# Splitting the loop of expert units in two: w_in in eight units, w_out three tiles at a time, and ten w_out tiles converted in the first token pair

## The chip, the cores and the metric

One core of one Trainium2 chip runs the whole program in one launch. The metric is the device time of one execution in microseconds. Before the change, three runs took 1532.82, 1535.92 and 1537.63 us, median 1535.92 us. The execution that was profiled took 1532.53 us, of which 1530.8 us lie between the first and the last instruction of the program.

## The reference, cut to what matters

The program computes three layers in sequence on 4608 tokens of width 512:

```python
x = attention(q, k, v)                 # keys and values averaged over 8 positions first
e = argmax(x @ w_gate + bias[modality])            # one of 8 experts for each token
x = gate * (relu(x @ w1[e]) @ w2[e])               # w1: 512x1024, w2: 1024x512, float32
h = x @ w_in                                       # w_in: 512x2048
out = (h * clip(h + 3, 0, 6) / 6) @ w_out          # w_out: 2048x512
```

`w_in` and `w_out` are float64 in memory. The kernel multiplies numbers as the sum of a high and a low float32 part with three products (high*high, high*low, low*high). So each float64 weight has first to be turned, with integer and float operations on its two 32-bit words, into two such parts. This is the conversion that the change moves about.

## The kernel before, in words

The work runs in three stages one after the other: the attention, which also routes each token's row to a list of its expert in device memory; the expert units (function `moe1`); and the last layer (function `moe2`).

An expert unit is 400 rows of one expert. The inputs of this case make twelve units. The first (`unit(0, first=True)`) and the last (`unit(..., last=True)`) are written out, the ten between them are one hardware loop whose count is read from a register (`nc.values_load(g.nun, ...)`, L1040, `tc.For_i`, L1041). A unit has eight steps `f`. Step `f` issues the load of the weight tile `f+3` (`w_dma`, L880 and L882, two transfers of 256 KB into one of two buffers `ws`), splits tile `f+2` into high and low parts (`w_split`: a cast `wh` on ACT and a subtraction `wl` on DVE, twice), multiplies tile `f` with the unit's rows (`h_mm`, 12 matmuls into `ph`, then `hi` on ACT and `lo` on DVE), and then the second product of the tile before (`y_mm`, 12 matmuls into `y`; every third of them reads `lo`). Steps 1 to 4 load the next unit's rows, POOL scales them one step later (`gate_x`, L863). In step 7 and behind it four column blocks of these rows are transposed on PE into `pt` and split into `xhi` (ACT) and `xlo` (DVE); the first block's bank also holds the tokens' numbers, which ACT copies to `tkr` (L876). `pt` has two banks, so the third transpose waits for the readers of the first: `xhi`, `xlo` and `tkr`.

Beside this, each of the ten loop units converts weights for the last layer. `conv` turns one half of a column chunk of `w_in` (`cs`, two transfers of 256 KB) into the seven sums `wq` of a Strassen scheme, in 13 operations, 2 of them on ACT and 11 on DVE; `conv_out` turns one of the sixteen tiles of `w_out` (`ds`, 512 KB) into `wv`, in 9 operations, 2 on ACT and 7 on DVE. A unit does two `conv` and one `conv_out`, 35 operations, handed out in order, five behind each of the steps 1 to 7:

```python
for _ in range(5):
    if ops:
        ops.pop(0)()
```

The results go to device memory: `wq` by L931 behind steps 4 and 6, `wv` by L1029 behind step 7. Which chunk and which tile a unit takes stands in rows 3 and 4 of the table `g.tab`: `min(i, 7)` for the chunk of `w_in` (there are eight, `NQ = 8`), `min(i, 9)` for the tile of `w_out` (`KD = 10`). With ten loop units the chunk 7 is therefore converted three times. These numbers are read into SP's registers at the start of a unit (L973, L974).

The last layer takes the tokens in six pairs of blocks (`j`), each in eight quads (`q`, one for each chunk of `w_in`). A quad (`quad`) has seven products `mm` of six matmuls into one of two PSUM banks `hps`, and between them the output matmuls (`o_group`, 36 in all) of the quad before; `rest(i)` behind product `i` issues what `extra[i]` holds, the next load of `sq` (`s_load`, 256 KB, seven ahead) and one or two of those groups. DVE adds what the Strassen scheme asks for (`vv`, `ww`, `c`) and makes `gl`; a product that goes on in a bank, or takes it anew, waits until DVE has read it. In the first pair (`j == 0`) one of the six `w_out` tiles that the loop did not convert is converted in each of the quads 0 to 5 (nine operations over `extra[0]` to `extra[4]`), and the other ten are fetched from device memory (`wo_get`, 512 KB each).

The order on PE, ACT, DVE and SP is the order in which the program text issues the operations; each engine works its queue in order, and SP issues nearly all transfers. An operation that waits holds up what stands behind it on its engine. A loop has no barrier between its iterations, but when it ends all engines wait for each other and SP waits for the loop's transfers.

Of the kernel before, what the change touches and what calls it, by code (L numbers as in the profile page):

```python
# [8 lines left out]
F32 = mybir.dt.float32  # L9
# [10 lines left out]
P = 128  # L20
# [21 lines left out]
KD = 10  # L42
# [612 lines left out]
def unit_consts(tc, g, c1):  # L655
# [29 lines left out]
    cv = f("ucv", 40)  # L685
    nc.gpsimd.tensor_scalar(cv[0:1], cw[0:1], float(KD - 1), None, op0=ALU.min)
    nc.gpsimd.tensor_scalar(cw[0:1], cw[0:1], float(NQ - 1), None, op0=ALU.min)
    g.tab = g.cp.tile([1, 5, 40], I32, name="tab")
# [3 lines left out]
    nc.gpsimd.tensor_copy(g.tab[:, 4, 1:40], cv[0:1, 0:39])  # L692
# [61 lines left out]
def unit_table(tc, g, new):  # L754
# [9 lines left out]
    v.tensor_scalar(g.nun, u.m[0:1], -2.0, None, op0=ALU.add)  # L764
# [49 lines left out]
def moe1(tc, g, xr_d, tok_d, y_d, s_d, v_d, w1, w2, w_in):  # L814
# [83 lines left out]
    def store_y(col):  # L898
        return nc.sync.dma_start(y_d.rearrange("(d p) n -> p d n", p=P)[:, :, bass.ds(col, NW)], s.yo)
# [25 lines left out]
    def conv_out(t):  # L925
        a, m, ex = (s.cv.tile([P, 4, P], I32, name=n, tag=n).rearrange("p k f -> p (k f)") for n in ("a", "m", "ex"))
        o = s.cv.tile([P, 2, DM], F32R, name="wv", tag="wv")
        return o, f64_split(nc, g, t[:, :, 1], t[:, :, 0], a, m, ex, o[:, 0], o[:, 1])
# [4 lines left out]
    def unit(i, first=False, last=False, tail=None):  # L933
# [29 lines left out]
        for f in range(8):  # L963
# [6 lines left out]
            if f == 0 and not first:  # L970
                col = reg(2, i, NT)
                if not last:
                    cc = nc.values_load(g.tab[0:1, 3, bass.ds(i, 1)], engines=(ET.SP,), min_val=0, max_val=NQ - 1)  # L973
                    cd = nc.values_load(g.tab[0:1, 4, bass.ds(i, 1)], engines=(ET.SP,), min_val=0, max_val=KD - 1)  # L974
# [20 lines left out]
            if last:  # L995
                if f in (1, 2):
                    g.y_load(0, f - 1)
                if f == 3:
                    ops = g.y_ops(0)
                if f >= 3:  # L1000
                    g.s_load()
                    for _ in range(3):
                        if ops:
                            ops.pop(0)()
                if f >= 6:
                    g.wo_load(KD + f - 6)
            elif not first:
                if f == 0:
                    cs[0], cs[1] = conv_load(cc, 0), conv_load(cc, 1)
                if f == 1:  # L1010
                    co, ops = conv(cs.pop(0))
                if f == 2:
                    cs[2] = g.wo_load(cd)
                if f == 3:
                    c1_, o_ = conv(cs.pop(1))
                    ops += o_
                if f == 5:
                    c2_, o_ = conv_out(cs.pop(2))
                    ops += o_
                for _ in range(5):  # L1020
                    if ops:
                        ops.pop(0)()
                if f == 4:
                    conv_store(co, cc, 0)
                if f == 6:
                    conv_store(c1_, cc, 1)
                if f == 7:
                    assert not ops
                    nc.sync.dma_start(v_d[bass.ds(cd, 1)].rearrange("o p x -> p (o x)"), c2_.bitcast(F32).rearrange("p w f -> p (w f)"))  # L1029
# [7 lines left out]
    def run(tail):  # L1037
        open_ps()
        unit(0, first=True, tail=tail)
        n_l = nc.values_load(g.nun, min_val=10, max_val=18)  # L1040
        with tc.For_i(0, n_l, 1, iteration_sync="reg_based") as i:  # L1041
            unit(i + 1)
        unit(n_l + 1, last=True)
        store_y(reg(2, n_l + 2, NT))
        es_p.close()
        es_l.close()
        es_r.close()
# [6 lines left out]
def moe2(tc, g, tok_d, v_d, out):  # L1054
# [23 lines left out]
    def wo_get(f):  # L1078
        nc.sync.dma_start(wo[f].bitcast(F32).rearrange("p w f -> p (w f)"), v_d[f])  # L1079
# [57 lines left out]
    def quad(j, q, groups, extra):  # L1137
# [29 lines left out]
        x = bank()  # L1167
# [20 lines left out]
    wo_get(NQ)  # L1188
    groups = []
    yo = []  # L1190
    for j in range(NP):
        for q in range(NQ):
            extra = {i: [] for i in range(7)}
            if j == 0:
                if q < KF - KD:
                    for n, op_ in enumerate(conv(KD + q)):
                        extra[n // 2].append(op_)
                if q < KF - KD - 2:
                    extra[6].append(lambda q=q: g.wo_load(KD + q + 2))
                for f in (q + 1, NQ + q + 1):  # L1200
                    if q < NQ - 1 and f < KD:
                        extra[3 if f < NQ else 4].append(lambda f=f: wo_get(f))
                if q == 1:
                    extra[0].append(lambda: v.tensor_copy(tki, tkf))  # L1204
            if j + 1 < NP:
# [23 lines left out]
def chunk_kernel(ctx, tc, q, k, v, mid, w_gate, mbias, w1, w2, w_in, w_out, out):  # L1229
# [7 lines left out]
    v_d = dp.tile([KD, P, 2 * DM], F32, name="vd")  # L1237
    s_d = dp.tile([NQ, 7, 2, P, 2 * P], F32, name="sd")
    with tc.manual_schedule(engines={ET.PE, ET.Activation, ET.DVE, ET.SP}):
# [50 lines left out]
        def wo_load(f):  # L1290
            t = g.yp.tile([P, DM, 2], I32, name="ds", tag="ds", bufs=2)
            src = w_out.bitcast(I32).rearrange("(f p) x -> f p x", p=P)[bass.ds(f, 1)]
            nc.sync.dma_start(t.rearrange("p f w -> p (f w)"), src.rearrange("o p x -> p (o x)"))
            if isinstance(f, int):
                g.sts[f] = t
            return t
# [36 lines left out]
```

## Time and profile before

| | |
|---|---|
| runs | 1532.82, 1535.92, 1537.63 us |
| profiled execution | 1532.53 us, span 1530.8 us |
| PE busy | 1421.2 us (93%) |
| DVE busy | 978.9 us (64%) |
| ACT busy | 624.2 us (41%) |
| POOL busy | 206.9 us (14%) |
| first transpose of a unit's tokens, ten loop units apart | 248.3 and 699.1 us |
| last layer's first product | 747.6 us |

PE is busy for most of the span in every stage, so a stretch is read by what PE waits for in it and at which clock it ran. The granted clock is given as a share: 1.00 is 2.4 GHz, 0.5 is 1.2 GHz.

### The profile page before, as it was taken

The page shows a single profiled execution, that of the slowest core. Times are in us where ns is not written, and L with a number is a line of the kernel's source. Part 1 is how long each engine was busy: PE and PEld are TensorE (multiplying, and loading weights), DVE is VectorE, ACT ScalarE, POOL GpSimd, SP SyncE. Part 2 cuts the span into 40 slices and gives each one's busy share as a digit, 9 for nine tenths or more (in the row PEclk, how much of TensorE's full clock was granted, in tenths as well). Part 3 has the DMA queues.
Part 4 walks back from the last instruction along what each step waited for, and adds up shares of the span by engine and source line. Part 5 has one row for each costly group of instructions (what it writes and reads, how often), then busy time and mean ns, then how long its engine had stood idle before and what let it go on. Part 6 is the DMA issues. An engine that isn't in the chain of part 4 may idle for free.

```text
span 1530.8 us, 24942 instructions
## 1 busy us (share of the span) xinstructions
PE 1421.2 (93%) x7673; PEld 1289.5 (84%) x7673; DVE 978.9 (64%) x1964; ACT 624.2 (41%) x1263; POOL 206.9 (14%) x233
## 2 busy tenths in 40 slices
PE   7898988889888889888899999999999999999998
PEld 6787877888888888888888888888888888888886
DVE  7898773877777887776667644554564464455443
ACT  3665643444444444344433433333343243333322
POOL 5654242111100111110000010010010001001001
PEclk8999998999999999999999999999999999999999
DMA  9973254776766677765775454355445335445442
GB/s 297 287 230 127 97 165 128 221 236 220 233 196 210 204 233 229 237 211 183 236 257 162 127 176 142 113 152 159 117 138 173 116 118 172 138 117 152 118 116 69
DMA packets 243142, 268.29 MB, mean 175 GB/s; under 512 B 25762, under 2 KB 203426, under 8 KB 243058
## 3 DMA queue, kind: packets, MB, share of 16 engines
q1 hardware_dynamic: 235858, 247.04, 53.1%
q0 software_dynamic: 7200, 20.18, 3.6%
q8 instruction: 47, 0.77, 0.2%
q14 instruction: 37, 0.30, 0.1%
HBM read 213.55 MB, written 61.01 MB: 179 GB/s over the span
## 4 chain that ended last, share of the span: by engine, by line
issue 48%; PE 3%; POOL 2%; DMA 0%; SPq 0%; POOLq 0%; ACT 0%; DVE 0%
POOL out_dram L1092 2%; PE ph L945 1%; PE y L958 1%; DMA sq<-sd 0%; SPq L1283 0%; PE hps L1113 0%; POOLq L1328 0%; SPq L1079 0%; ACT dex L795 0%; POOLq L1092 0%; ACT s L1153 0%; SPq L1184 0%; DVE dm L796 0%; DVE tki L1204 0%
## 5 line engine op out<-in xcount | busy, mean ns | idle before, releaser
L1113 PE MATMUL hps<-yc,sq 128*128 128x384 f32 x2016 | 412.6, 339 | 11.7 <-DVE c L1134 6.6
L1113 PEld LDWEIGHTS hps<-yc,sq 128*128 128x128 f32 x2016 | 364.1, 188 | 47.3 <-DVE c L1134 13.7
L1103 PE MATMUL ops<-wo,gh 128*128 128x512 f32 x1152 | 361.5, 394 | 0.0
L1103 PEld LDWEIGHTS ops<-wo,gh 128*128 128x128 f32 x1152 | 212.4, 187 | 22.9
L1103 PE MATMUL ops<-wo,gl 128*128 128x512 f32 x576 | 227.9, 396 | 0.0
L787 DVE TENSOR_TENSOR wl<-ws,wh 128x512 fp32r<-128x512 f32 x192 | 139.3, 755 | 77.1 <-ACT wh L786 69.0
L1124 ACT ACTIVATE r<-c,three 128x384 f32<-128x384 f32 x144 | 88.8, 617 | 220.0 <-DVE c L1134 219.0
L786 ACT CAST wh<-ws 128x512 fp32r<-128x512 f32 x192 | 114.5, 619 | 118.0 <-DMA ws<-in_moe_w_dram 108.5
L958 PE MATMUL y<-lo,wh 128*128 128x400 f32 x384 | 143.1, 373 | 20.1 <-DVE lo L950 19.9
L958 PE MATMUL y<-hi,wh 128*128 128x400 f32 x384 | 141.9, 370 | 8.4 <-ACT hi L949 8.3
L1128 ACT CAST gh<-r 128x384 fp32r<-128x384 f32 x192 | 98.5, 513 | 122.4 <-DVE r L1125 122.4
L1092 POOL DMA_INDIRECT out_dram<-osb,tki x36 | 35.3, 980 | 799.1 <-ACT osb L1090 768.7
L958 PE MATMUL y<-hi,wl 128*128 128x400 f32 x384 | 138.7, 361 | 0.0
L945 PE MATMUL ph<-xhi,wh 128*128 128x400 f32 x384 | 133.9, 349 | 2.6 <-PEq L1328 1.8
L945 PE MATMUL ph<-xlo,wh 128*128 128x400 f32 x384 | 133.8, 348 | 0.0
L945 PE MATMUL ph<-xhi,wl 128*128 128x400 f32 x384 | 133.4, 347 | 0.0
L1103 PEld LDWEIGHTS ops<-wo,gl 128*128 128x128 f32 x576 | 107.7, 187 | 26.1
L1129 DVE TENSOR_TENSOR gl<-r,gh 128x384 fp32r<-128x384 f32 x192 | 106.4, 554 | 31.5 <-ACT gh L1128 27.2
L1125 DVE SCALAR_TENSOR_TENSOR r<-r,c 128x384 f32<-128x384 f32 x144 | 80.4, 558 | 56.6 <-ACT r L1124 54.3
L863 POOL TENSOR_TENSOR cxg<-cxg 100x512 f32<-100x512 f32 x48 | 59.9, 1250 | 410.3 <-DMA cxg<-xr 204.5
L958 PEld LDWEIGHTS y<-lo,wh 128*128 128x128 f32 x384 | 77.2, 201 | 32.7 <-DVE lo L950 32.6
L1125 DVE SCALAR_TENSOR_TENSOR r<-r,hps 128x384 f32<-128x384 f32 x48 | 26.6, 554 | 97.8 <-ACT r L1124 97.8
(229 smaller groups left out, 1970.5 us busy)
## 6 DMA issues: line engine op xcount, KB each, us to landing
sq<-sd SPq DMA_DIRECT2D x336, 256.0 KB
ws<-in_moe_w_dram SPq DMA_DIRECT2D x192, 256.0 KB, 4.6
sd<-wq SPq DMA_DIRECT2D x20, 896.0 KB, 5.7
cs<-in_moe_w_in_dram SPq DMA_DIRECT2D x40, 256.0 KB, 3.6
cxg<-xr SPq DMA_DIRECT2D x44, 225.8 KB
yd<-yo SPq DMA_DIRECT2D x12, 800.0 KB, 7.3
yr<-yd SPq DMA_DIRECT2D x12, 768.0 KB
kv<-in_k_dram SPq DMA_DIRECT2D x16, 512.0 KB
```

Source lines behind the costliest of these rows:

```text
L786: nc.scalar.copy(hi, src)
L787: nc.vector.tensor_tensor(lo, src, hi.bitcast(F32), op=ALU.subtract)
L863: nc.gpsimd.tensor_tensor(s.xg[:, t, 0:DM].rearrange("p (h x) -> p h x", x=D), v, s.xg[:, t, GC:GC + 1].unsqueeze(2).to_broadcast([T4, H, ...
L945: nc.tensor.matmul(ph, a[j][:, 0, k * P:(k + 1) * P], b[k], start=(n == 0), stop=(n == 11))
L958: nc.tensor.matmul(yps[d], a[j][:, 1, d * P:(d + 1) * P], b, start=(f == 0 and n == 0), stop=(f == 7 and n == 2))
L1092: i_ = nc.gpsimd.indirect_dma_start(out=out, out_offset=bass.IndirectOffsetOnAxis(ap=tki[:, c:c + 1], axis=0), in_=o, in_offset=None).ins
L1103: nc.tensor.matmul(pso[t_], gt[a][:, t * P:(t + 1) * P], wo[f][:, b], start=(q == 0 and fh == th and n == 0), stop=(q == NQ - 1 and fh != ...
L1113: nc.tensor.matmul(ps, w[:, kk, a * P:(a + 1) * P], y[:, b, kk], start=(start and n == 0), stop=(n == 5), skip_group_check=True)
L1124: a_.activation(r, c, AF.Relu, bias=g.three)
L1125: v.scalar_tensor_tensor(r, r, 6.0, c, op0=ALU.min, op1=ALU.mult)
L1128: a_.copy(gh, r)
L1129: late.append(lambda: v.tensor_tensor(gl, r, gh.bitcast(F32), op=ALU.subtract))
```

## The change

The one loop becomes two. The first has eight iterations, a constant, and its units do two `conv` each with the loop's own counter as the chunk; they convert no `w_out` tile. Their operations start behind steps 1 and 4, five a step, and the stores stand behind steps 4 and 7. The second loop has as many iterations as units are left (two here); its units do no `conv` and three `conv_out` each, four operations a step, with the loads at steps 0 to 2 and the stores behind steps 3, 5 and 7; the first such unit takes tiles 0 to 2, all later ones tiles 8 to 10. The register with the second loop's count is read between the loops. The other ten `w_out` tiles are converted in the first token pair, two operations at each of the seven places of a quad, nine places a tile. The first quad's third product takes a third PSUM bank, that of an output tile.

```diff
-KD = 10
+KD = 3
...
-    nc.gpsimd.tensor_scalar(cv[0:1], cw[0:1], float(KD - 1), None, op0=ALU.min)
-    nc.gpsimd.tensor_scalar(cw[0:1], cw[0:1], float(NQ - 1), None, op0=ALU.min)
+    nc.gpsimd.tensor_scalar(cw[0:1], cw[0:1], float(NQ + 1), None, op0=ALU.is_ge)
...
-    v.tensor_scalar(g.nun, u.m[0:1], -2.0, None, op0=ALU.add)
+    v.tensor_scalar(g.nun, u.m[0:1], -2.0 - NQ, None, op0=ALU.add)
...
-        o = s.cv.tile([P, 2, DM], F32R, name="wv", tag="wv")
+        o = s.cv.tile([P, 2, DM], F32R, name="wv", tag="wv", bufs=2)
...
                 if not last:
-                    cc = nc.values_load(g.tab[0:1, 3, bass.ds(i, 1)], engines=(ET.SP,), min_val=0, max_val=NQ - 1)
-                    cd = nc.values_load(g.tab[0:1, 4, bass.ds(i, 1)], engines=(ET.SP,), min_val=0, max_val=KD - 1)
+                    cc = quad
+                    if quad is None:
+                        cd = nc.values_load(g.tab[0:1, 3, bass.ds(i, 1)], engines=(ET.SP,), min_val=0, max_val=1)
...
-                    g.wo_load(KD + f - 6)
-            elif not first:
+                    g.wo_load(KD + NQ * (f - 6))
+            elif quad is not None:
                 if f == 0:
                     cs[0], cs[1] = conv_load(cc, 0), conv_load(cc, 1)
                 if f == 1:
                     co, ops = conv(cs.pop(0))
-                if f == 2:
-                    cs[2] = g.wo_load(cd)
-                if f == 3:
-                    c1_, o_ = conv(cs.pop(1))
-                    ops += o_
-                if f == 5:
-                    c2_, o_ = conv_out(cs.pop(2))
-                    ops += o_
+                if f == 4:
+                    c1_, ops = conv(cs.pop(1))
                 for _ in range(5):
                     if ops:
                         ops.pop(0)()
                 if f == 4:
                     conv_store(co, cc, 0)
-                if f == 6:
+                if f == 7:
                     conv_store(c1_, cc, 1)
-                if f == 7:
-                    assert not ops
-                    nc.sync.dma_start(v_d[bass.ds(cd, 1)].rearrange("o p x -> p (o x)"), c2_.bitcast(F32).rearrange("p w f -> p (w f)"))
+            elif not first:
+                if f < KD:
+                    cs[f] = g.wo_load(cd, f)
+                if 1 <= f <= KD:
+                    co, o_ = conv_out(cs.pop(f - 1))
+                    ops += o_
+                    cs[8 + f] = co
+                for _ in range(4):
+                    if ops:
+                        ops.pop(0)()
+                if f > 0 and f % 2 == 1 and f // 2 in range(1, KD + 1):
+                    n = f // 2
+                    nc.sync.dma_start(v_d[bass.ds(cd, 1), n - 1].rearrange("o p x -> p (o x)"),
+                                      cs.pop(8 + n).bitcast(F32).rearrange("p w f -> p (w f)"))
...
-        n_l = nc.values_load(g.nun, min_val=10, max_val=18)
+        with tc.For_i(0, NQ, 1, iteration_sync="reg_based") as i:
+            unit(i + 1, quad=i)
+        n_l = nc.values_load(g.nun, min_val=2, max_val=10)
         with tc.For_i(0, n_l, 1, iteration_sync="reg_based") as i:
-            unit(i + 1)
-        unit(n_l + 1, last=True)
-        store_y(reg(2, n_l + 2, NT))
+            unit(i + NQ + 1)
+        unit(n_l + NQ + 1, last=True)
+        store_y(reg(2, n_l + NQ + 2, NT))
...
-        x = bank()
+        x = bank() if j or q else ps_o.tile([P, DM], F32, name="ops5", tag="o5")[:, 0:TB]
         mm(j, x, 3, True)
...
+    fs = [h * NQ + f for f in range(KD, NQ) for h in range(2)]
+    cops = []
+    for n, f in enumerate(fs):
+        o_ = []
+        cops += [lambda f=f, o_=o_: (o_.extend(conv(f)), o_.pop(0)())] + [lambda o_=o_: o_.pop(0)()] * 5
+        if n + 2 < len(fs):
+            cops.append(lambda f=fs[n + 2], o_=o_: (o_.pop(0)(), g.wo_load(f)))
+        cops += [lambda o_=o_: o_.pop(0)()] * (9 - len(cops) % 9 if len(cops) % 9 else 0)
...
             if j == 0:
-                if q < KF - KD:
-                    for n, op_ in enumerate(conv(KD + q)):
-                        extra[n // 2].append(op_)
-                if q < KF - KD - 2:
-                    extra[6].append(lambda q=q: g.wo_load(KD + q + 2))
-                for f in (q + 1, NQ + q + 1):
-                    if q < NQ - 1 and f < KD:
-                        extra[3 if f < NQ else 4].append(lambda f=f: wo_get(f))
+                for i in range(7):
+                    for _ in range(2):
+                        if cops:
+                            extra[i].append(cops.pop(0))
                 if q == 1:
                     extra[0].append(lambda: v.tensor_copy(tki, tkf))
+                if q < KD - 1:
+                    extra[3].append(lambda q=q: wo_get(q + 1))
+                    extra[4].append(lambda q=q: wo_get(NQ + q + 1))
```

The table loses its fifth row, and the buffer of converted `w_out` tiles in device memory is indexed by half and tile (`[2, KD, ...]`).

## Rows read from the trace of the kernel before

**Rows 1.** The page's first part: engine, busy us (share), instructions.

```profile
PE 1421.2 (93%) x7673; PEld 1289.5 (84%) x7673; DVE 978.9 (64%) x1964; ACT 624.2 (41%) x1263; POOL 206.9 (14%) x233
```

**Rows 2.** Instructions on the next unit's rows: count, ns min/median/max, first and last start.

```profile
L873 PE MATMUL pt<-idn,cxg x11: 249/249/374, 248.3 to 699.1; 100*4 100x100 f32 x11
```

**Rows 3.** PE's waits, 250 to 712 us: total us, times, longest.

```profile
PE pt L871 <- ACT tkr L876: 20.8, 10, 2.1
PE y L958 <- DVE lo L950: 19.3, 31, 1.0
PE y L958 <- ACT hi L949: 8.3, 7, 2.5
PE pt L871 <- DVE xlo L787: 3.8, 8, 0.5
PE ph L945 <- PEq L1328: 1.8, 1, 1.8
```

**Rows 4.** Stretches: busy us of each engine (count), granted clock, DMA share, GB/s.

```profile
299.00:303.00 4.00, 4.00 (x16) 3.96 (x15) 3.86 (x7) 1.01 (x3) 0.00 (x0) 0.57 0.31 125
...
711.00:716.00 5.00, 4.90 (x18) 4.91 (x19) 1.87 (x3) 1.65 (x3) 0.00 (x0) 0.66 0.44 136
716.00:747.00 31.00, 31.00 (x172) 31.00 (x172) 20.46 (x29) 14.69 (x25) 0.00 (x0) 1.00 0.67 218
```

**Rows 5.** The same view, one loop unit.

```profile
654.00:699.00 45.00, 39.13 (x210) 37.24 (x209) 33.83 (x60) 19.47 (x38) 5.40 (x4) 0.96 0.70 219
```

**Rows 6.** PE in order of time at a unit's end: start, us, instruction.

```profile
388.07 1.96 PE L871 MATMUL pt<-idn,cxg 100*128 100x100 f32 x8 [2.09 <-ACT tkr L876]
...
390.54 0.54 PE L958 MATMUL y<-lo,wh 128*128 128x400 f32 x1
```

**Rows 7.** DVE in order of time at that unit's end.

```profile
382.81 1.08 DVE L922 TENSOR_TENSOR wq<-wx,wq 128x896 fp32r<-128x896 f32 x1
383.81 0.42 DVE L796 TENSOR_SCALAR m<-ex 128x512 f32<-128x512 f32 x1
384.26 0.43 DVE L797 TENSOR_SCALAR m<-m 128x512 int32<-128x512 int32 x1
384.78 0.75 DVE L798 SCALAR_TENSOR_TENSOR a<-ds,sgn,m 128x512 int32<-128x512 int32 x1
385.45 1.28 DVE L787 TENSOR_TENSOR wl<-ws,wh 128x512 fp32r<-128x512 f32 x2
...
387.14 0.56 DVE L787 TENSOR_TENSOR xlo<-pt,xhi 128x400 fp32r<-128x400 f32 x1
```

**Rows 8.** ACT in order of time, same place.

```profile
387.78 0.23 ACT L876 COPY tkr<-pt 4x100 f32<-4x100 f32 x1 [3.39 <-issue]
```

**Rows 9.** SP's transfers in order of time, into the next unit.

```profile
391.75 0.37 SPq L1029 DMA_DIRECT2D vd<-wv  x1
394.38 0.39 SPq L880 DMA_DIRECT2D ws<-in_moe_w_dram  x1
...
397.88 2.33 SPq L904 DMA_DIRECT2D cs<-in_moe_w_in_dram  x4
```

**Rows 10.** ACT's waits, 250 to 712 us.

```profile
ACT wh L786 <- DMA ws<-in_moe_w_dram: 77.2, 62, 3.0
```

**Rows 11.** DVE in order of time, while POOL scales rows.

```profile
274.61 2.14 DVE L787 TENSOR_TENSOR wl<-ws,wh 128x512 fp32r<-128x512 f32 x2
```

**Rows 12.** POOL in order of time, same place.

```profile
275.04 1.15 POOL L863 TENSOR_TENSOR cxg<-cxg 100x512 f32<-100x512 f32 x1 [1.64 <-PE ph L945]
```

**Rows 13.** PE in order of time where the loop is entered.

```profile
258.04 0.45 PE L945 MATMUL ph<-xhi,wh 128*128 128x400 f32 x1 [0.65 <-ACTq L1041]
```

**Rows 14.** The line that reads the loop's count: PE's instruction.

```profile
L1040 PEldq TENSOR_LOAD <-nun x1: 487/487/487, 254.1 to 254.1; - x1
```

**Rows 15.** Loop control, 240 to 720 us: PE's hint behind each branch.

```profile
L1328 PEldq BRANCH_PREFETCH_HINT  x10: 31/31/41, 255.8 to 660.4; - x10
```

**Rows 16.** Stretches of the last layer's first pair, columns as in group 4.

```profile
762.00:778.00 16.00, 16.00 (x80) 14.34 (x81) 9.62 (x20) 5.00 (x10) 0.00 (x0) 1.00 0.88 300
...
809.00:825.00 16.00, 16.00 (x81) 14.29 (x80) 11.73 (x22) 6.09 (x12) 0.00 (x0) 1.00 0.57 188
```

**Rows 17.** PE's waits over the span, last layer.

```profile
PE hps L1113 <- DVE c L1134: 6.6, 5, 1.3
...
PE hps L1113 <- DMA sq<-sd: 4.6, 2, 2.5
...
PE hps L1113 <- DVE r L1125: 0.3, 1, 0.3
```

More of the change, by code (lines that the diff above doesn't have):

```diff
@@ L684, in unit_consts @@
     io(cw[0:1], [[1, 40]])
-    cv = f("ucv", 40)
-    nc.gpsimd.tensor_scalar(cv[0:1], cw[0:1], float(KD - 1), None, op0=ALU.min)
-    nc.gpsimd.tensor_scalar(cw[0:1], cw[0:1], float(NQ - 1), None, op0=ALU.min)
-    g.tab = g.cp.tile([1, 5, 40], I32, name="tab")
+    nc.gpsimd.tensor_scalar(cw[0:1], cw[0:1], float(NQ + 1), None, op0=ALU.is_ge)
+    g.tab = g.cp.tile([1, 4, 40], I32, name="tab")
     nc.gpsimd.memset(g.tab, 0)
@@ L691, in unit_consts @@
     nc.gpsimd.tensor_copy(g.tab[:, 3, 1:40], cw[0:1, 0:39])
-    nc.gpsimd.tensor_copy(g.tab[:, 4, 1:40], cv[0:1, 0:39])
     g.nun = g.cp.tile([1, 1], I32, name="nun")
@@ L931, in conv_store, with unit @@
         nc.sync.dma_start(s_d[bass.ds(c, 1), :, h].rearrange("o s p x -> p (o s) x"), o.bitcast(F32).rearrange("p s w f -> p s (w f)"))
-    def unit(i, first=False, last=False, tail=None):
+    def unit(i, first=False, last=False, tail=None, quad=None):
         e = s.e0 if first else reg(0, i, E - 1)
@@ L1078, in wo_get @@
     def wo_get(f):
-        nc.sync.dma_start(wo[f].bitcast(F32).rearrange("p w f -> p (w f)"), v_d[f])
+        nc.sync.dma_start(wo[f].bitcast(F32).rearrange("p w f -> p (w f)"), v_d[f // NQ, f % NQ])
     tkf = c1.tile([P, NT // P], F32, name="tkf")
@@ L1236, in chunk_kernel @@
     y_d = dp.tile([DM, NT + NW], F32, name="yd")
-    v_d = dp.tile([KD, P, 2 * DM], F32, name="vd")
+    v_d = dp.tile([2, KD, P, 2 * DM], F32, name="vd")
     s_d = dp.tile([NQ, 7, 2, P, 2 * P], F32, name="sd")
@@ L1288, in chunk_kernel, with wo_load @@
         g.sts = {}
-        def wo_load(f):
+        def wo_load(f, k=None):
             t = g.yp.tile([P, DM, 2], I32, name="ds", tag="ds", bufs=2)
-            src = w_out.bitcast(I32).rearrange("(f p) x -> f p x", p=P)[bass.ds(f, 1)]
-            nc.sync.dma_start(t.rearrange("p f w -> p (f w)"), src.rearrange("o p x -> p (o x)"))
-            if isinstance(f, int):
+            src = w_out.bitcast(I32).rearrange("(h f p) x -> h f p x", h=2, p=P)
+            src = src[f // NQ, f % NQ] if k is None else src[bass.ds(f, 1), k].rearrange("o p x -> p (o x)")
+            nc.sync.dma_start(t.rearrange("p f w -> p (f w)"), src)
+            if k is None:
                 g.sts[f] = t
```

## The prediction

> **What bounds the kernel now.** I read the busy shares first, then the waits of the busiest engine, then the order of time at the places where they fall. PE is busy for 93% of the span, DVE for 64% [rows 1]; so the time is PE's, and a change gains only where PE waits or runs at a low clock. The first transposes of two neighbouring units stand at 248.3 and 699.1 us, eleven in count [rows 2], so a loop unit takes 450.8 / 10 = 45.1 us. PE's waits in that stretch are 20.8 + 19.3 + 8.3 + 3.8 = 52.2 us, 5.2 a unit [rows 3]. The reader is to see that nearly all of them are for DVE or for ACT behind DVE: the third transpose waits once in every unit for `tkr`, 2.1 us; the second products wait for `lo`.
>
> The clock adds to this. Behind the wait at a unit's end the granted clock is 0.57 over 4 us, which costs 4 x 0.43 = 1.7 us, and the one unit in the middle of the table has 0.96 over 45 us, 1.8 us [rows 4, 5]. The matmuls show it: 0.54 us each in the low spell [rows 6]. The last unit converts nothing in its steps and from 716 to 747 us PE is busy all the time at clock 1.00 [rows 4]. So a loop unit without waits and spells would take about 45.1 - 5.2 - 1.8 = 38.1 us.
>
> Why does `tkr` come late? ACT sat idle 3.4 us before it [rows 8] and starts at 387.78, where DVE's `xlo` of the same bank ends (387.14 + 0.56) [rows 7]. DVE in turn had worked since 382.81 without a pause: `wq`, then three operations of the `w_out` tile, then the split of step 7, `lo`, `xlo`. It was late by what the conversion had put ahead. SP is late by the same cause: its store of `wv` stands at the end of the unit's queue, goes out at 391.75, and the next unit's weight load at 394.38 and its `w_in` loads at 397.88 stand behind it [rows 9]. ACT waits 77.2 us for weights in this stretch, 62 times [rows 10], and where it does, `hi` stands behind the cast.
>
> **A unit of the first loop.** It loses one `conv_out` of 9 operations, 7 on DVE, at 0.42 to 0.75 us [rows 7], 2.9 to 5.3 us, some 4 us of the 33.8 that DVE is busy in a unit [rows 5]. What matters is where. Four terms:
>
> (a) The unit's end. Behind step 6 DVE now has `wq` 1.08, `m` 0.42 and 0.43, `a` 0.75 = 2.68 us of conversion [rows 7]. In the new order step 6 holds the last three operations of the second `conv`: one small sum, a cast on ACT, and `wq`, about 1.08 + 0.3 on DVE and some wait for the cast. That is 1.3 us less ahead of `xlo`. Behind step 7 stands nothing, so the third and fourth `xlo` come early too. The wait is 20.8 / 10 + 3.8 / 10 = 2.5 us a unit. I take 1.4 off; ends 0 (the cast's wait eats it) and 2.5.
>
> (b) `lo`. 19.3 / 10 = 1.9 us a unit. Steps 3 and 4 give up operations (the second `conv` starts behind step 4, not 3), and DVE starts the unit without a debt. I take 1.2 off; ends 0 and 1.9. Against a larger value: POOL's row scaling comes four times a unit whatever is converted, and while it runs two `wl` take 2.14 us [rows 11, 12] against 1.28 [rows 7]. The Trainium skill (SBUF — State Buffer, "SBUF: two separate sides") says that DVE with two SBUF inputs and a GpSimd operation that reads SBUF lock a shared port pair for a whole instruction, the loser blocked; the 0.86 us between the two rows agrees. By that rule alone these waits would mostly stay, and the sum below would be some 6 us smaller.
>
> (c) `hi`. 8.3 / 10 = 0.8 us a unit. The last transfer in a unit's SP queue is now the `wq` store of step 7, whose data is ready behind step 6: 383.9 us in the unit shown, where `wv` held SP until 391.75 [rows 7, 9]. SP also reads two registers fewer and issues no `ds` load between the weight loads. I take 0.7 off; ends 0 and 0.8.
>
> (d) The clock. The low spells follow the long waits. If the wait at the unit's end falls under 1.2 us, I expect most to go: 1.1 of the 1.7 us [rows 4]; ends 0 and 1.7.
>
> Sum 1.4 + 1.2 + 0.7 + 1.1 = 4.4 us a unit, ends 0 and 6.9; eight units: -35.2 us (0 to -55).
>
> **A unit of the second loop.** Three `conv_out` put 21 operations on DVE instead of 29, but behind step 6 stand about as many as now, step 7 still has some, and the last store of `wv` holds SP as it does now. I take 0.7 us a unit off, -1.4 for two (0 to -4). The third `ds` load waits on SP for a DVE operation of step 2; behind it stands the weight load of step 3, which in turn waits for DVE's split of that step, so I put it at nothing; without that cover ACT would wait for the weights by up to 3 us, the longest such wait [rows 10], inside these ends' other side (+6).
>
> **The border between the loops.** Leaving a loop costs a wait of all engines: PE 1.8 us [rows 3], then a low spell, 0.34 x 5 = 1.7 us [rows 4]. Entering costs 0.65 us now [rows 13], because PE's queue is full of matmuls while its sequencer reads the count (254.1 us) and steps to the branch hint (255.8), 1.7 us [rows 14, 15]. At the new border the queue is empty, so I take the 1.7 us in full less 0.1: 1.8 + 1.7 + 1.6 = +5.1 us; ends 1.8 + 0.65 = 2.5 and 8 (SP's first load of the second loop late as well, by the 3 us of [rows 10]).
>
> **The first token pair.** Four more tiles: 28 operations on DVE, at the 0.42 to 0.75 us above 12 to 21 us, over eight quads 1.5 to 2.6 a quad. DVE is busy 11.7 of 16 us in a full quad [rows 16]; 14 us at most is still under PE's 16, and in those quads PE has no wait. The cover is DVE's slack; where it was short in the later pairs a wait for `c` was 1.3 us [rows 17]. I take 0.3 us; ends 0 and 8 x 1.3 = 10.4. Transfers: the second quad moves 300 GB/s already, at a DMA share of 0.88 [rows 16], and gets one more tile from each source, 1 MB in 16 us, 63 GB/s. 300 / 0.88 = 341 is less than 363, so a `sq` load may be late; the waits for them are 2.1 and 2.5 us now [rows 17]. I take +1.2 (0 to 3). The third bank takes off the one wait for `r`, 0.3 us [rows 17].
>
> **The sum** on the profiled execution: -35.2 - 1.4 + 5.1 + 0.3 + 1.2 - 0.3 = -30.3 us, so 1532.5 - 30.3 = 1502.2. The median of the runs lies 3.4 us above that execution, and I predict the median: 1535.9 - 30.3 = 1505.6, said as 1506.
>
> **The rivals.**
>
> 1. Only the early part gains. `tkr` stays behind `xlo`, which stays behind the split of step 7 and `lo`; if the cast of `wq` on ACT makes DVE wait as long as the three operations took that are gone, the wait at the end stays at 2.1 us, and with it the spells. For it: ACT's cast stands behind `hi` in its queue. Against it: DVE's row shows no pause to be filled. Then (b) and (c) alone, 1.9 us a unit: -15.2 - 1.4 + 6.3 = -10.3, 1526 us. Chance 0.17.
>
> 2. Slower. The pace of a unit is set by the weights' own chain (load, cast, `wl`, `lo`, `xlo`) and not by the conversion, so that the eight units gain nothing. For it: ACT waits for weights 62 times [rows 10], and a unit that takes less time asks for the same bytes sooner. Against it: the last unit, which has that chain and other work on DVE, has no wait at all from 716 to 747 us [rows 4]. Then the border and the first pair alone count: +5.1 + 1.2 = +6.3, 1542 us. It decides if a unit gains less than 6.3 / 8 = 0.8 us. Chance 0.08.
>
> 3. All waits go. DVE is never late, PE runs the first loop as it runs the last unit: the upper ends, -55 - 1.4 + 6.3 = -50, 1486 us. For it: the rows of the last unit [rows 4]. Against it: POOL's four locks and the border of a step on DVE [rows 11]. Chance 0.15.
>
> 4. The first pair becomes DVE's: the conversion's 14 places a quad put two operations ahead of every `c`, and seven quads wait as the worst does now: 7 x 1.3 = 9 us on top of the sum, 1515. Chance 0.10.
>
> 5. The change does not do what it says: if there were fewer than two units for the second loop, tiles would be missing. The trace has ten loop units [rows 2], so the second loop has two, and it takes each half once. No chance worth a number.
>
> **How the numbers follow.** The forecast has 0.50 (1498 to 1514). A measurement of this kernel can tell about 0.3%, 4.6 us, from no change: 1531.3 to 1540.5. Faster are the forecast, rivals 1, 3 and 4, less a little of rival 1's upper side: 0.89; slower is most of rival 2: 0.06; the same 0.05. The range of 1486 to 1528 takes in rivals 1, 3 and 4 and leaves out rival 2, half of the far end of 3, and the slow side of 1.
>
> **What would show it.** Right: the wait of `pt` for `tkr` in the first loop under 1.2 us a unit, `y` for `hi` gone there, SP's first weight load of a unit issued before that unit's first product, granted clock of most units 0.98 or more, a unit of the first loop about 40.7 us from transpose to transpose and one of the second about 44.4; a single wait of PE of 3 to 4 us between the loops. In the first pair PE stays busy for the whole of the third and later quads. Wrong: units of 43 us or more with `tkr` unchanged (rival 1), units of 45 (rival 2), waits for `c` in the first pair in quad after quad (rival 4), or a border of more than 8 us.

## The result, and the profile after

The changed kernel takes 1480.97 us (median of 4 runs, 1478.56 to 1482.01) beside 1536.33 for the kernel before; the ratio is 0.9641, 95% interval 0.9621 to 0.9661. The forecast of 1506 had the sign right and the size wrong by nearly half: 55 us came off, not 30, and the time lies under the lower end of the range.

The profiled execution has a span of 1478.6 us, 52.2 less than before. All but 0.4 us of it lies in four pieces, each read from the starts of the units' token transposes (247.9 to 638.5 us after, [rows 2] before), from the first product of the last layer (688.4 us after, 747.6 before) and from the span:

| | before | after | difference |
|---|---|---|---|
| eight units of the first loop | 8 x 45.08 = 360.6 | 299.1 | -61.5 |
| two units behind them, border included | 90.2 | 91.5 | +1.3 |
| last unit | 48.5 | 49.9 | +1.4 |
| last layer | 783.2 | 790.2 | +7.0 |

The page's first part, with [rows 1] beside it: PE is 21 us less busy with the same instructions, DVE 31 us less.

```profile
PE 1400.0 (95%) x7673; PEld 1282.2 (87%) x7673; DVE 948.0 (64%) x1920; ACT 622.8 (42%) x1255; POOL 204.1 (14%) x231
```

The marks of the first loop's units (line, engine, operation, count, ns, first and last start): seven units in 546.9 - 288.1 = 258.8 us, 37.0 each. The first two of the eight units take 40.3 and 40.0, the other six 36.4 to 36.7.

```profile
L870 PEld LDWEIGHTS pt<-idn,cxg x8: 85/85/85, 288.1 to 546.9; 100*4 100x4 f32 x8
```

PE's waits from 285 to 690 us, the answer to [rows 3]. From 295 to 540 us the same view has no row: PE waits for nothing in the six units from the third on. But for 1.5 us at the first unit's end, the large rows that are left stand behind the first loop: the 3.4 us put down to `issue` at the border, the 3.4 us put down to PE's sequencer at the end of the second loop, where [rows 3] has 1.8, and the rest in the units between.

```profile
PE pt L868 <- ACT tkr L873: 8.7, 3, 5.4
PE ph L942 <- issue: 3.4, 1, 3.4
PE ph L942 <- PEq L1341: 3.4, 1, 3.4
PE y L955 <- ACT hi L946: 2.5, 2, 1.3
```

The stretches that answer to [rows 4, 5]: one first-loop unit, the border, the second unit of the second loop, and the front of the last layer. PE is busy throughout at clock 1.00 in the first; the other three have spells at the low clock.

```profile
401.00:437.00 36.00, 36.00 (x208) 35.94 (x207) 29.35 (x51) 18.73 (x35) 4.86 (x4) 1.00 0.78 245
556.00:562.00 6.00, 5.83 (x24) 5.83 (x25) 2.78 (x5) 2.43 (x5) 0.00 (x0) 0.72 0.45 106
597.00:605.00 8.00, 4.61 (x18) 4.28 (x19) 5.60 (x10) 2.65 (x6) 0.00 (x0) 0.57 0.16 66
697.00:711.00 14.00, 10.27 (x30) 9.21 (x31) 7.21 (x15) 4.46 (x8) 0.00 (x0) 0.51 0.98 336
```

A unit's end, in order of time, three views of the same microseconds. DVE first, to be held against [rows 7]: between `lo` of step 6 and `xlo` there is now a pause of 1.01 us for ACT's cast and no `w_out` operation, and `xlo` follows on `lo` without a wait.

```profile
398.89 1.09 DVE L919 TENSOR_TENSOR wq<-wx,wq 128x896 fp32r<-128x896 f32 x1 [1.01 <-ACT wq L918]
399.89 1.29 DVE L784 TENSOR_TENSOR wl<-ws,wh 128x512 fp32r<-128x512 f32 x2
401.51 0.57 DVE L947 SCALAR_TENSOR_TENSOR lo<-ph,hi 128x400 fp32r<-128x400 f32 x1 [0.33 <-ACT hi L946]
402.00 0.57 DVE L784 TENSOR_TENSOR xlo<-pt,xhi 128x400 fp32r<-128x400 f32 x1
```

PE: the third and fourth block's transposes (eight instructions) start at 403.73 without a wait, where [rows 6] has 2.09 us; `tkr` was copied at 402.65. The next unit's first product starts at 406.60.

```profile
403.73 0.85 PE L868 MATMUL pt<-idn,cxg 100*128 100x100 f32 x8
...
406.60 0.35 PE L942 MATMUL ph<-xhi,wh 128*128 128x400 f32 x1
```

SP: the last store of the unit goes out at 400.01 and the next unit's first weight load at 402.86, 3.7 us ahead of the product above. In [rows 9] that load stood at 394.38, 1.6 us behind PE's first product of its unit (the last line here, from the trace before). The loads lead by 5.3 us more.

```profile
400.01 0.40 SPq L928 DMA_DIRECT2D sd<-wq  x1
402.86 0.39 SPq L877 DMA_DIRECT2D ws<-in_moe_w_dram  x1
403.67 0.34 SPq L879 DMA_DIRECT2D ws<-in_moe_w_dram  x1
405.16 2.11 SPq L901 DMA_DIRECT2D cs<-in_moe_w_in_dram  x4
```

```profile
392.81 0.34 PE L945 MATMUL ph<-xhi,wh 128*128 128x400 f32 x1
```

### The profile page after: what moved, and what is told of

Same layout as the page of the kernel before. It is cut to its first block, busy times and chain, and to the rows that moved or that the text cites. A ratio compares the mean times of both kernels' runs of the same rounds, so it can differ in the third digit from the quotient of the medians.

```text
span 1478.6 us, 24692 instructions
## 1 busy us (share of the span) xinstructions
PE 1400.0 (95%) x7673; PEld 1282.2 (87%) x7673; DVE 948.0 (64%) x1920; ACT 622.8 (42%) x1255; POOL 204.1 (14%) x231
## 4 chain that ended last, share of the span: by engine, by line
issue 50%; PE 3%; POOL 2%; DMA 1%; DVE 0%; POOLq 0%; ACT 0%; SPq 0%; ACTq 0%
POOL out_dram L1097 2%; PE ph L942 1%; PE y L955 1%; DMA sq<-sd 1%; PE hps L1118 0%; POOLq L1341 0%; ACT r L1129 0%; DVE r L1130 0%; DVE c L1139 0%; DVE da L795 0%; DVE dm L797 0%; POOLq L1097 0%; DVE gl L1134 0%; SPq L1189 0%; DVE dex L796 0%
## 5 line engine op out<-in xcount | busy, mean ns | idle before, releaser
L1118 PE MATMUL hps<-yc,sq 128*128 128x384 f32 x2004 | 411.9, 340 | 14.7 <-DVE c L1139 7.3
L784 DVE TENSOR_TENSOR wl<-ws,wh 128x512 fp32r<-128x512 f32 x192 | 131.7, 719 | 60.4 <-ACT wh L783 53.1
L955 PE MATMUL y<-hi,wh 128*128 128x400 f32 x384 | 136.6, 356 | 2.6 <-ACT hi L946 2.5
L955 PE MATMUL y<-lo,wh 128*128 128x400 f32 x384 | 135.3, 352 | 1.8 <-DVE lo L947 1.8
L955 PE MATMUL y<-hi,wl 128*128 128x400 f32 x384 | 133.9, 349 | 0.0
L1108 PEld LDWEIGHTS ops<-wo,gl 128*128 128x128 f32 x576 | 108.0, 188 | 26.3
L1129 ACT ACTIVATE r<-hps,three 128x384 f32<-128x384 f32 x48 | 27.9, 581 | 136.7 <-PE hps L1118 136.6
L1130 DVE SCALAR_TENSOR_TENSOR r<-r,hps 128x384 f32<-128x384 f32 x48 | 26.6, 553 | 90.2 <-ACT r L1129 90.1
```

Source lines behind the costliest of these rows:

```text
L784: nc.vector.tensor_tensor(lo, src, hi.bitcast(F32), op=ALU.subtract)
L955: nc.tensor.matmul(yps[d], a[j][:, 1, d * P:(d + 1) * P], b, start=(f == 0 and n == 0), stop=(f == 7 and n == 2))
L1108: nc.tensor.matmul(pso[t_], gt[a][:, t * P:(t + 1) * P], wo[f][:, b], start=(q == 0 and fh == th and n == 0), stop=(q == NQ - 1 and fh != ...
L1118: nc.tensor.matmul(ps, w[:, kk, a * P:(a + 1) * P], y[:, b, kk], start=(start and n == 0), stop=(n == 5), skip_group_check=True)
L1129: a_.activation(r, c, AF.Relu, bias=g.three)
L1130: v.scalar_tensor_tensor(r, r, 6.0, c, op0=ALU.min, op1=ALU.mult)
```

## The experiments

Two theories stood for the first loop. **S**: the store of `wv`, which waits for the last operation of the unit, holds SP's in-order queue and with it the next unit's loads; late loads make ACT's casts late, these `hi` and `wl`, and these `lo`, `xlo` and `tkr`. **D**: the nine `conv_out` operations themselves, ahead of `lo` and `xlo` on DVE, make the waits. The first three runs take each apart from the other.

### The store moved, all work kept (kernel before)

```diff
             if f == 3 and not first:
                 store_y(col)
+                cp = reg(4, prev, KD - 1)
+                nc.sync.dma_start(v_d[bass.ds(cp, 1)]..., s.wv...)
...
-                if f == 7:
-                    nc.sync.dma_start(v_d[bass.ds(cd, 1)]..., c2_...)
```

What is stored there is the tile of the unit before; the buffer `wv` is kept across units for it.

> The kernel before with one thing moved: the wv store of a unit no longer ends the unit's SP queue, it goes out behind step 3 of the next unit; DVE and ACT do all they did. Theory S (the store, which waits for wv, holds SP and so the next unit's loads, and the waits of PE follow from late loads): loop units fall from 45.1 us to 37 to 39 us, ten of them, total 1465 to 1475 us. Theory D (the nine conv_out operations on DVE ahead of lo and xlo make the waits): units stay at 44 us or more, the 2.1 us wait for tkr at each unit's end stays, total 1522 to 1536 us.

Measured: 1488.88 us, ratio 0.9721 (0.9693 to 0.9749). Eleven marks from 248.0 to 652.8 us, 40.5 us a unit.

```profile
L875 PEld LDWEIGHTS pt<-idn,cxg x11: 85/85/124, 248.0 to 652.8; 100*4 100x4 f32 x11
```

PE's waits from 295 to 540 us, to be held against [rows 3], which cover ten units. `hi` has gone from the list, `lo` is at 0.2 us; `tkr` is left at 1.5 us a unit, with DVE's 29 operations unchanged.

```profile
PE pt L873 <- ACT tkr L878: 10.7, 7, 2.1
PE pt L873 <- DVE xlo L787: 3.1, 7, 0.5
PE y L960 <- DVE lo L952: 0.2, 1, 0.2
```

So moving one store, with nothing taken off any engine, gives 44 us beside the 55 of the change. It gives them in ten units, 4.6 us each, where the change's first loop gains 7.7 in each of eight. S holds; its number was missed by 14 us, since I had left no share to D or to anything else on SP's queue.

### SP held again, light DVE (changed kernel)

```diff
             for c in range(2, 4):
                 transp(c, ps())
+            if quad is not None:
+                hd = s.cv.tile([P, 1], F32, name="hd", tag="hd")
+                nc.vector.tensor_copy(hd, s.xlo[3][:, 0:1].bitcast(F32))
+                nc.sync.dma_start(g.hold_d, hd)
```

> The changed kernel with one thing added to the eight units of the first loop: a copy of 128 values on DVE behind the last xlo and a store of them (512 bytes) at the end of the unit's SP queue, so that SP is held about as long as by the wv store before. Theory S: the first loop's units go from 36.4 us back to 42 to 45 us, total 1525 to 1545 us. Theory D: they stay under 37.5 us, total 1479 to 1489 us.

Measured: 1541.05 us, ratio to the kernel before 1.0058 (1.0035 to 1.0081). The first loop's units are back at (600.2 - 286.5) / 7 = 44.8 us:

```profile
L870 PEld LDWEIGHTS pt<-idn,cxg x8: 84/85/85, 286.5 to 600.2; 100*4 100x4 f32 x8
```

ACT's and then PE's waits from 295 to 540 us. ACT waits 76 us for weights, 29 times, up to 7.4 us; PE waits for `hi`, which stands behind those casts.

```profile
ACT wh L783 <- DMA ws<-in_moe_w_dram: 76.0, 29, 7.4
```

```profile
PE y L955 <- ACT hi L946: 18.2, 7, 3.5
PE pt L868 <- ACT tkr L873: 5.4, 5, 1.2
PE pt L868 <- DVE xlo L784: 2.4, 5, 0.5
PE y L955 <- DVE lo L947: 2.1, 7, 0.7
```

SP in order of time at a unit's end: the 512 bytes go out at 383.47, the first weight load at 385.69.

```profile
377.94 0.40 SPq L928 DMA_DIRECT2D sd<-wq  x1
383.47 0.34 SPq L1039 DMA_DIRECT2D hold<-hd  x1
385.69 0.40 SPq L877 DMA_DIRECT2D ws<-in_moe_w_dram  x1
```

A transfer of 512 bytes, with a copy of 128 values on DVE to feed it, costs 60 us of the total because of where it waits. D is excluded as the main cause: DVE had its light load here.

### DVE's work put back, SP free (changed kernel)

```diff
-                if f == 4:
-                    c1_, ops = conv(cs.pop(1))
+                if f == 3:
+                    t1 = cs.pop(1)
+                    c1_, o_ = conv(t1)
+                    ops += o_
+                if f == 5:
+                    x_, o_ = conv_out(t1.rearrange("p k f w -> p (k f) w"))
+                    ops += o_
```

> The changed kernel with the nine conv_out operations back in the eight units of the first loop, at the places that they had before (second conv from step 3, conv_out from step 5), on words of w_in that are in the buffer anyway; their result is not stored and nothing is added to SP's queue. Theory D: the first loop's units go from 36.4 back to 42 to 45 us, total 1525 to 1545 us. Theory S: under 38.5 us, the 29 DVE operations fit, total 1479 to 1495 us.

The result `x_` is stored nowhere. Measured: 1494.28 us, ratio 0.975 (0.972 to 0.9781), 13 us over the changed kernel; units of (564.3 - 292.3) / 7 = 38.9 us, near what S said. PE's waits from 295 to 540 us are those of the first experiment, at a unit's end alone:

```profile
PE pt L868 <- ACT tkr L873: 7.8, 7, 2.1
PE pt L868 <- DVE xlo L784: 3.1, 7, 0.5
```

Together, one first-loop unit in us (mean of seven; of all ten in the kernel before):

| | 29 DVE operations | 22 DVE operations |
|---|---|---|
| SP held at the end | 45.1 (before) | 44.8 (second run) |
| SP free | 38.9 (third run) | 37.0 (after) |

D is worth 1.9 us where SP is free and 0.3 us where it is held; S is worth 6.2 and 7.8. The step from 45.1 to 38.9 takes along whatever else the change does on SP's queue; the first run, which moves the one store alone, is worth 4.6.

### The store of `wq` back behind step 6 (changed kernel)

```diff
-                if f == 7:
+                if f == 6:
                     conv_store(c1_, cc, 1)
```

> The changed kernel with the store of the second wq back behind step 6, ahead of the weight loads of step 7, where it stood before. It waits for wq, the last operation of step 6. If every store that waits at its place in SP's queue costs: the first loop's units go from 36.4 to 37.5 to 39 us, total 1488 to 1502 us. If only the hold at the unit's end costs (a weight buffer is not free before DVE has split it, so step 7's load waits anyway): units within 0.5 us, total 1478 to 1485 us.

Measured: 1489.67 us, ratio 0.9692 (0.9667 to 0.9717); units of (554.9 - 291.1) / 7 = 37.7 us. The total is 8.7 us longer, but the first loop accounts for only 5.1 of that in the trace (304.2 us for its eight units beside 299.1): the six units from the third on take 37.5 us instead of 36.5. So a store that waits for something nearly ready, ahead of one pair of loads, costs about 1 us in each of these, and part of the gain of S is this second move of the diff, which the prediction did not price. The rest of the 8.7 us lies outside the first loop, 4.4 of it in the unit across the border; what makes it was not tried.

### The border by itself (kernel before, its loop cut in two)

```diff
-        n_l = nc.values_load(g.nun, min_val=10, max_val=18)
+        with tc.For_i(0, NQ, 1, iteration_sync="reg_based") as i:
+            unit(i + 1)
+        n_l = nc.values_load(g.nun, min_val=2, max_val=10)
         with tc.For_i(0, n_l, 1, iteration_sync="reg_based") as i:
-            unit(i + 1)
+            unit(i + NQ + 1)
```

> The kernel before with its loop cut in two, eight and two units, the body the same in both: the border by itself. The estimate of 5.1 us (1.8 wait of all engines, 1.6 uncovered loop setup, 1.7 low clock) gives 1538 to 1539 us beside 1533 to 1534; with a pause of DVE of 3 us at the first pass through the second body 1541 to 1542. Rival: the border also frees SP of the held store once, and the gain of that eats it, 1533 to 1536 us.

Measured: 1546.97 us beside 1535.23, ratio 1.007 (1.0044 to 1.0096), so 6.8 to 14.7 us. More than the estimate; the runs spread from 1540 to 1548, and the profiled one is the fastest of them, so what the others add was not seen. In its trace the unit across the border takes 52.3 us, 7.2 more than a unit of the kernel before. PE waits 3.25 us there, and the low clock that begins with the wait at the unit's end lasts across the border to 624 us, which costs 5.58 x 0.47 + 5.00 x 0.49 = 5.1 us:

```profile
609.70:619.00 9.30, 5.58 (x21) 4.86 (x21) 5.00 (x9) 3.12 (x7) 0.00 (x0) 0.53 0.35 121
619.00:624.00 5.00, 5.00 (x15) 4.95 (x16) 1.29 (x2) 1.28 (x3) 0.00 (x0) 0.51 0.05 13
```

### The token load moved (changed kernel, then kernel before)

```diff
-    nc.sync.dma_start(tkf, tok_d[0:NT].rearrange("(c p) -> p c", p=P))
...
+                if q == 4:
+                    extra[6].append(lambda: nc.sync.dma_start(tkf, tok_d[0:NT].rearrange("(c p) -> p c", p=P)))
-                if q == 1:
+                if q == 6:
                     extra[0].append(lambda: v.tensor_copy(tki, tkf))
```

> The changed kernel with the load of the token numbers (4608 pieces of 4 bytes) moved from the front of the last layer to the end of the fifth quad of the first pair. Theory T (this load holds SP's next issue, 5.3 us in the trace after, and the two waits for sq of 4.0 and 2.7 us and the low clock behind them follow): both waits go or fall under 0.5 us, the last layer's time from first product to end falls from 790 to 779 to 783 us, total 1469 to 1474 us. Rival (the fetched and raw w_out tiles take the transfers' time): the waits stay within 1 us of what they are, total 1478 to 1483 us.

> The kernel before with the late token load alone. Theory T: its two waits for sq (2.1 and 2.5 us) and the low clock behind them (1.7 us) go, total 1527 to 1531 us. Rival (those waits are the fetched tiles' own): within 2 us of the kernel before.

Measured: 1473.96 us, ratio 0.9626 (0.9599 to 0.9653), for the changed kernel, and 1526.67, ratio 0.9952 (0.9933 to 0.997), for the one before: 7 us off either. The last layer's own time falls from 790.2 to 1471.5 - 688.3 = 783.2, and from 783.2 to 1526.0 - 746.7 = 779.3. What the load does is seen in the trace after, SP in order of time; two `sq` issues take 5.8 us behind it:

```profile
689.63 0.45 SPq L1189 DMA_DIRECT2D tkf<-tokd  x1
690.13 5.80 SPq L1295 DMA_DIRECT2D sq<-sd  x2
```

Theory T holds for the time; it was too sharp for the waits: of the two waits in the changed kernel one of 2.0 us is left, with one of 0.5 elsewhere.

### The first pair's conversion one quad later (changed kernel)

```diff
-                        if cops:
+                        if cops and q > 0:
```

> The changed kernel with the first pair's conversion started one quad later, so that the first quad loads no third raw tile and converts nothing; the token load stays in front. Theory W (the first pair's 7 us more come from the change's own transfers beside the token load, DMA share 0.98 at 336 GB/s against 0.89 before): first product to end falls from 790 to 784 to 786 us, total 1475 to 1478. Rival (the token load alone, whatever else is there): within 1.5 us of the changed kernel, 1479 to 1482.

Measured: 1480.37 us, ratio 0.9651 (0.9635 to 0.9667), no gain. PE's waits for `sq` stand at 6.3 us (6.7 before this edit), and the low clock stays at 0.53 from 697 to 711 us. Theory W falls: the first quad's conversion is not what makes its loads late.

```profile
PE hps L1118 <- DVE c L1139: 7.8, 7, 1.8
PE hps L1118 <- DMA sq<-sd: 6.3, 2, 4.1
```

### Five operations a step in the second loop, and all three

```diff
                 if f < KD:
                     cs[f] = g.wo_load(cd, f)
...
-                for _ in range(4):
+                for _ in range(5):
                     if ops:
```

> The kernel with the late token load, and in the second loop's two units five conversion operations a step instead of four, so that the third tile is done behind step 6 and its store no longer holds SP behind step 7. Theory S for the second loop: the unit behind such a store and the last unit lose the waits of the held loads, from the third-last mark to the first product of the last layer 141 us become 132 to 137, total 1464 to 1470 us. Rival (these units are slow by the border, by a 3 us pause of DVE at the first pass through the new code and by five operations more of DVE in early steps): total 1472 to 1478 us.

> Late token load, five operations a step, conversion from the second quad on, all together. If the three gains are apart from each other: 1460 to 1468 us. If conversion from the second quad on pushes DVE into the quad with the next pair's differences: waits for c of 1.3 us and more in quad 7, 1468 to 1476.

With the late token load and five a step: 1467.39 us (1466.3 to 1470.9), ratio 0.9578 (0.9558 to 0.9597), the fastest version here. From the last mark of the first loop to the last layer's first product it takes 680.0 - 543.8 = 136.2 us instead of 141.4 (140.8 with the late token load alone). The third tile is done earlier, and its store goes out 4.0 us behind the unit's mark (592.4, mark 588.4) instead of 9.8 (603.0, mark 593.2, in the first of the two token-load runs). With the conversion from the second quad on as well, 1472.28 us, ratio 0.9604 (0.9588 to 0.962): 5 us worse, with a wait for `c` of 1.8 us in the eighth quad, where the next pair's differences come. So the three edits are not apart from each other: the third, without a gain alone, costs here.

## Why the prediction was wrong

**What held.** PE's waits and low spells were where the gain lay, and they stood where [rows 3] puts them. `tkr`, `hi` and `lo` went; every sign that was named for the first loop came, at a larger size. The objection that POOL's row scaling would keep `lo` late did not come: PE's waits for `lo` are 0.7 us from 285 to 690 us, with POOL's scaling as before. Rival 2 (the weights' own chain sets the pace) is excluded by the first run; of rival 3 the mechanism was right, six of the first loop's eight units run without a wait, though its 1486 us were still too many. Against the sum, the eight units gained 26.3 us more than forecast (61.5 beside 35.2), and the last layer gave 5.8 of that back.

**The step that failed is term (c).** It saw that SP is held by `wv` until 391.75 and that SP's release comes 8 us earlier [rows 7, 9], and then priced that release by the waits for `hi` alone, 0.8 us a unit at the most. The waits for `lo` and `tkr`, and the spells behind them, were given to the conversion on DVE in terms (a), (b) and (d). The table of four says otherwise: with SP held, taking the operations off DVE gains 0.3 us a unit, and with the operations left on DVE, freeing SP gains 6.2. Term (c) had 0.7; (a), (b) and (d) had 3.7, and the operations on DVE turned out to be worth 1.9 where SP is free. The `w_in` loads, which the prediction itself names as standing behind the store, were given no price. How the hold becomes three rows of waits can be followed in the unit before the one shown in [rows 6 to 9], from the views of SP, ACT and DVE:

```profile
346.05 0.37 SPq L1029 DMA_DIRECT2D vd<-wv  x1
352.18 2.33 SPq L904 DMA_DIRECT2D cs<-in_moe_w_in_dram  x4
356.44 0.67 ACT L795 ACTIVATE ex<-cs 128x512 f32<-128x512 f32 x1 [3.17 <-DMA cs<-in_moe_w_in_dram]
357.13 0.43 DVE L796 TENSOR_SCALAR m<-ex 128x512 f32<-128x512 f32 x1 [3.00 <-ACT ex L795]
```

DVE stands idle for 3 us because the `w_in` words are not there, and its conversion starts late; from 360 us to the unit's end at 388 it has only two stops of over 1 us (1.17 and 1.53) and works off that debt, with `lo`, `xlo` and `tkr` behind it. In a unit of the first, the third and the changed kernel's trace no such stop for `w_in` words is left. The view of waits names the last link of a chain, so one cause stood in three rows. That the store is the cause is shown by the runs; the way through DVE is read from the traces, and with the light load of the second run the same hold showed for the most part as waits for `hi`. The Trainium skill (Perfetto Trace Analysis, "DMA Optimizations") says that, especially where there are loops, it may make sense to give input loads to one engine and output stores to another. No run here does that; the first run, in which loads no longer stand behind such a store on the same queue, agrees so far as that took 4.6 us off a unit.

**The other error is the pace without waits.** The prediction took 45.1 - 5.2 - 1.8 = 38.1 us and bounded the gain by 6.9; the first loop's undisturbed units take 36.4 to 36.7 (their token transposes start at 364.6, 401.1, 437.5 and 474.2 us on PE in the trace after). Idle time in the view of waits is less than what a wait costs. In the trace before, around one wait for `lo`:

```profile
276.27 0.34 PE L958 MATMUL y<-hi,wl 128*128 128x400 f32 x1
277.28 0.45 PE L958 MATMUL y<-lo,wh 128*128 128x400 f32 x1 [0.68 <-DVE lo L950]
277.57 0.34 PE L958 MATMUL y<-hi,wh 128*128 128x400 f32 x1
277.75 0.34 PE L958 MATMUL y<-hi,wl 128*128 128x400 f32 x1
```

Unbroken matmuls start 0.18 us apart and last 0.34, so they overlap. Across the wait the starts lie 1.01 us apart: it costs 1.01 - 0.18 = 0.83 us, 0.15 more than the 0.68 of the row, and the next start comes 0.11 us late as well. With 31 + 10 + 8 + 7 waits in ten units [rows 3] that is 5.6 x 0.26 = 1.5 us a unit if each is like this one, most of the 1.7 that were missing. Counted from the other side it would have been found: 192 matmuls at 0.182 us and 17 transposes in about 1.5 us are 36.4.

**The second loop and the border.** The border came out as the estimate: PE waits 3.43 us (1.8 + 1.6 had been taken), and 6 us at clock 0.72 cost 1.7. That it met so closely is in part luck: in the kernel before, with a wait and its low spell just ahead of the border, the same cut cost more. The units behind it were put at 44.4. The first takes 45.1 with the border, so 40.0 without, which was not foreseen; its first weight load goes out at 557.18, 1.0 us behind its first product (556.16), so SP does not lead there either, and why it is shorter stays open. The second takes 46.4, so that the two together came near the forecast by errors that offset each other. In it DVE stops for 3 us with nothing to wait for, and `tkr` comes late by that:

```profile
593.96 0.69 DVE L797 SCALAR_TENSOR_TENSOR m<-ds,ex 128x512 f32<-128x512 uint32 x1
597.65 1.29 DVE L784 TENSOR_TENSOR wl<-ws,wh 128x512 fp32r<-128x512 f32 x2 [3.00 <-issue]
```

```profile
600.28 1.96 PE L868 MATMUL pt<-idn,cxg 100*128 100x100 f32 x8 [5.38 <-ACT tkr L873]
```

From 594.6 to 597.7 us the transfers hold one packet of instructions, and no other unit of this trace has such a stop on DVE:

```profile
q14 instruction: 1, 0.01, 0.7%
```

A stop of DVE with nothing to wait for, of 1.0 to 3.1 us, stands in the first pass of the second loop in all nine traces with two loops, and none of 1 us or more in the units of the three with one. That it is DVE's code at its first pass fits this, but was not tried by itself. That the store of `wv` holds SP in these units too was right; the run with five operations a step took 4.6 us off this stretch, though it moves DVE's work forward as well.

**The first pair.** Predicted +1.2, measured +7.0. DVE's slack sufficed, as forecast: waits for `c` grow from 6.6 to 7.3 us over the whole last layer. The waits for `sq` are 6.7 us instead of 4.6, and the low spell behind them runs through all of 697 to 711 us (clock 0.51), which costs 10.27 x 0.49 = 5.0 us of PE's busy time, where it cost 3.40 x 0.34 = 1.2 before:

```profile
756.00:761.00 5.00, 3.40 (x12) 2.89 (x12) 4.08 (x8) 2.39 (x5) 0.00 (x0) 0.66 0.90 292
```

So 3.8 us of the 7.0 are the clock, 2.1 the waits for `sq` and 0.7 those for `c`. The reason given for late loads, bytes of the second quad, is not borne out: the waits end at 698.0 and 704.9 us, ahead of the first quad's sixth product and the second quad's first; without the first quad's conversion nothing changes, and with the token load moved 2.0 us of them are left. Both kernels hold their `sq` loads behind the token load. The long spell is not the change's own: the first experiment, whose last layer is the old one, has it too, and there the last layer takes 1486.8 - 699.6 = 787.2 us.

```profile
707.00:721.00 14.00, 10.35 (x29) 9.32 (x30) 5.95 (x13) 4.43 (x8) 0.00 (x0) 0.51 1.03 351
```

The old last layer takes 783.2, 787.2 and 786.3 us in three traces (before, the first run, the loop cut in two), the new one 790.2, 787.9, 786.7 and 788.3 in four (after, and the second, third and fourth run): 2.7 us apart in the mean. With the token load out of the way the two are 783.2 - 779.3 = 3.9 us apart, one trace each. So the change's own part is, as an estimate, some 3 to 4 of the 7 us; the rest is how these two executions happened to fall, and why the clock stays low for longer in one than in the other stays open.

## What to carry to other kernels

Where one engine issues loads and stores in order, look at what each store waits for, not at its bytes: a store at the end of a loop body that waits for the body's last result takes the prefetch away from the next iteration, and the price shows as waits on quite other engines. Before the waits of a view are shared out among causes, follow one of them back past the engine that it names, to the first thing in the iteration that was late. And work out the pace without waits from instructions times their undisturbed distance; subtracting idle time left it 1.7 us a unit too slow here.

## What was not expected of the hardware

A load of 4608 pieces of 4 bytes holds the next issue on its queue: the `sq` issue behind it took 5.3 us of the 5.8 shown in the trace after. Cutting a loop in two cost the kernel before 11.7 us in the medians (6.8 to 14.7), more than the 7.2 us by which the unit across the border is longer in the trace of its fastest run, where the wait and the low spell are of that size. And the low clock behind a like pair of waits at the front of the last layer cost 1.2 us in the kernel before (4.6 us of waits) and 10.35 x 0.49 = 5.1 us in the first experiment (4.8 us of waits).
